# Recurrent attention and expert layers in one kernel: where the probabilities are loaded, and which engines do three small steps of the first unit

## The chip, the cores and the metric

The kernel runs on one core of one Trainium2 chip. The metric is the device time of one execution in microseconds (us), taken as the median of several runs. A core has five engines, each with its own in-order queue: PE (TensorE: matmuls; its weight loads are listed as PEld), DVE (VectorE), ACT (ScalarE), POOL (GpSimd) and SP (SyncE, which here only issues DMAs). DMAs from all queues run on the same 16 DMA engines.

## The reference

```python
# q, k, v, alpha: (4, 8, 768, 48) = batch, heads, time, head_dim
for t in range(S):
    state = alpha[:, :, t, :, None] * state + np.einsum('bhd,bhe->bhde', k[:, :, t], v[:, :, t])
    y[:, :, t] = np.einsum('bhd,bhde->bhe', q[:, :, t], state)
x = y.transpose(0, 2, 1, 3).reshape(3072, 384)
p = domain_probs / (domain_probs.sum(-1, keepdims=True) + 1e-09)      # (3072, 4)
for e in range(4):
    h = np.maximum(x @ w1[e], 0.0)                                    # w1[e]: 384 x 1024
    out += p[:, e:e + 1] * (h @ w2[e])                                # w2[e]: 1024 x 384
```

All is float32. A gated recurrence gives `x`; four expert layers are then applied to every row of it, and added with normalized probabilities as weights.

## The kernel before, in words

**Units.** The recurrence is cut into units of one batch and 128 time steps: 24 units, in the order of `units`. The generator `attention(u)` (L273) emits one unit in steps, one for each `yield`. Group 0 holds units 0 and 1; the later groups hold four each. When the units of a group are done, the expert layers run over their rows: `up` (L538 for group 0, L546 later) multiplies by `w1`, `down` (L637) by `w2`.

**One unit.** Alpha, k and q are loaded as rows (128 time steps on the partitions) and turned by PE transposes (L270, PSUM tile `tp`) into `AT` (copied by ACT, L281), `KT` (ACT, L286) and `QT`, which DVE multiplies by `AT` while reading PSUM (L293). The *own terms* are each step's product with itself: `t = q*k` (L289) and its sum over a head, `dot` (L290), which DVE writes onto the diagonal of `near` (L364). Then seven levels follow, for blocks of 1, 2, 4 ... 64 steps. In a level, `copy_q` copies the odd halves of `QT` into a block `qb` (two ACT copies, L312), `next_q` decays these halves in `QT` (DVE, L319) and forms the decays of the next level (DVE, L321), and `next_k` copies the odd halves of `KT` into the tile of the next level (L330, one copy of 128x256) while DVE writes the decayed even halves beside them (L331). The last level, 64, has no copy in `next_k`. PE forms the products of a level (`sc`, L338; `far`, L393, for level 64) and DVE takes them into `near` under a mask (`take`, L348). At the end `lat` is put together: two copies from `far` (ACT, L406), then two from `near` (ACT, L410), one for each half of the partitions. PE multiplies `lat` with the values (`yps`, L432), ACT copies the result into `xT` (L448), and PE forms the state for the next time steps from the turned keys (`turn_keys`, L456; `sps`, L467).

**Order at the start.** The order is written out by hand (`tc.manual_schedule()`, L721): every engine runs its instructions in the order in which they are emitted. ACT first issues three DMAs (L722 to L724): the identity, the masks, and the probabilities (`p_all`). SP issues the inputs of units 0 and 1 (`load(0, "akqv")`, `load(1, "akqv")`: a, k and q in one DMA each, L167, 192 KB; v in three, L172 to L174), then four pieces of the first expert's `w1` (`load_piece`, three DMAs each, L214 and L215). POOL clears tiles (L725 to L733). Then the steps of units 0 and 1 are emitted from a list of pairs (unit, n): one step of that unit, and `fill(n)` behind it, which puts n matmuls of zeros on PE (L747; each is two PE instructions). They need nothing that is still loading, and nothing reads what they give. `norm_probs` (L257 to L261) comes behind the list, and then the first `up`, for unit 0 alone. `load(after, ...)` inside a unit reloads its input tiles for a later unit; for unit 0 that is unit 2.

**Later.** A planner (`deal`, `cost`, `advance`) gives the steps of all later units due times among the matmuls of the expert layers; the change leaves it as it is.

Of the kernel before, what the change touches and what calls it, by code (L numbers as in the profile page):

```python
# [10 lines left out]
F32 = mybir.dt.float32  # L11
# [5 lines left out]
AX = mybir.AxisListType  # L17
# [3 lines left out]
def kernel(  # L21
# [37 lines left out]
    nc = tc.nc  # L59

    B, H, S, D = q.shape
    E, DM, F = moe_w1.shape
    P = 128
# [7 lines left out]
    NT = B * P  # L71
# [11 lines left out]
    n = np.arange(QUAD)[None, :]  # L83
# [7 lines left out]
    work = ctx.enter_context(tc.tile_pool(name="work", bufs=2))  # L91
# [7 lines left out]
    p_all = const.tile([P, NBLK, E], F32, name="p_all")  # L99
# [3 lines left out]
    near = const.tile([P, H, HALF], F32, name="near")  # L103
    lat = const.tile([P, H, P], F32, name="lat")
# [26 lines left out]
    def raw(u, nm):  # L131
        return values[u % 2] if nm == "v" else apart[nm] if u == 1 else early[nm]
# [27 lines left out]
    def load(u, names):  # L160
        if u >= len(units):
            return
        cb, b = units[u]
        for nm in names:
            src = srcs[nm][b, :, cb * P:(cb + 1) * P, :].rearrange("h s d -> s h d")
            if nm != "v":
                nc.sync.dma_start(out=raw(u, nm)[:, :, :D], in_=src)  # L167
                continue

            pairs = raw(u, nm).rearrange("p (a i) d -> p a i d", i=2)  # L170
            src = src.rearrange("p (a i) d -> p a i d", i=2)
            nc.sync.dma_start(out=pairs[:, :, 0, :D], in_=src[:, :, 0])  # L172
            nc.sync.dma_start(out=pairs[:, :, 1, :TAIL], in_=src[:, :, 1, QUAD:])
            nc.sync.dma_start(out=pairs[:, :, 1, TAIL:D], in_=src[:, :, 1, :QUAD])  # L174
# [13 lines left out]
    def load_piece(l, i, beside=False):  # L188
        if i >= E * NQ * LAST:
            return  # L190
        gi, k = divmod(i, E * NQ)
        e, c = divmod(k, NQ)
        if gi > l:
            w = wt[l][i] = wts.tile([P, 3, KC * QF], F32R, name=f"w{l + 1}",
                                    bufs=AHEAD if l == 0 else NQ)
            nc.sync.dma_start(out=w.bitcast(F32), in_=kept[l][k])
            return
        if l == 1 and not beside:
            return
        if l == 0:  # L200

            if gi > 0 or e == 0:
                shared[c] = wts.tile([P, 3, KC * QF], F32R, name="w2", bufs=NQ)
            w = shared[c][:, 2 - e % 2 if gi == 0 else 2].bitcast(F32)
        else:

            place = (hidden[c][:, 0] if not split2(gi, e, c) else hidden[c + NQ // 2][:, 1])
            w = place.rearrange("p f n -> p (f n)")[:, :KC * QF].bitcast(F32)
        wt[l][i] = w
        if l == 0:  # L210
            heads = moe_w1[e].rearrange("(h d) f -> h d f", d=D)[:, :, c * QF:(c + 1) * QF]
            w = w.rearrange("p (c f) -> p c f", f=QF)
            for part in range(2):
                nc.sync.dma_start(out=w[:, part], in_=heads[part * H // 2:(part + 1) * H // 2, :QUAD])  # L214
            nc.sync.dma_start(out=w[:, 2], in_=heads[:, QUAD:])  # L215
        else:
            nc.sync.dma_start(
                out=w.rearrange("p (c d) -> p c d", d=DM),
                in_=moe_w2[e].rearrange("(c p) d -> p c d", p=P)[:, c * FPQ:(c + 1) * FPQ])
# [44 lines left out]
    def halves(t, m):  # L264
        return t.rearrange("p a (b two r) -> p a b two r", two=2, r=m)

    def turned(src):
        tp = ps.tile([P, NP, P], F32, name="tp", tag="w")
        for p in range(NP):
            nc.tensor.transpose(tp[:, p, :], src(p), ident)  # L270
        return tp

    def attention(u):  # L273
        cb, b = units[u]
        ra, rk, rq, rv = (raw(u, nm) for nm in ("a", "k", "q", "v"))
# [6 lines left out]
        after = u + 2 if u == 0 else u + 1 if u > 1 else len(units)  # L282
# [1 line left out]
        yield  # L284
        KT = keys()
        nc.scalar.copy(out=KT, in_=turned(pair(rk)))  # L286
        own = work.tile([P, NT], F32, name="t")[:, :H * D].rearrange("p (h d) -> p h d", d=D)
        dot = work.tile([P, H], F32, name="dot")
        nc.vector.tensor_mul(own, rq[:, :, :D], rk[:, :, :D])  # L289
        nc.vector.reduce_sum(out=dot, in_=own, axis=AX.X)  # L290
        load(after, "k")
        yield
        nc.vector.tensor_mul(QT, turned(pair(rq)), AT)  # L293
        load(after, "q")
        yield

# [27 lines left out]
        def next_k(li):  # L324
            m = LEVELS[li]
            old = new = halves(KTs[li], m)
            if li + 1 < len(LEVELS):
                KTs.append(keys())
                new = halves(KTs[-1], m)
                nc.scalar.copy(out=new[:, :, :, 1, :], in_=old[:, :, :, 1, :])  # L330
            nc.vector.tensor_mul(new[:, :, :, 0, :], old[:, :, :, 0, :],  # L331
                                 spread(halved(decs[li])[:, :, :, 1], m))

# [70 lines left out]
        for s in range(2):  # L404
            rows = slice(HALF * s, HALF * (s + 1))
            nc.scalar.copy(out=parts[:HALF, :, s, :, HALF:], in_=far[rows])  # L406
        yield
        for s in range(2):
            rows = slice(HALF * s, HALF * (s + 1))
            nc.scalar.copy(out=lat[rows, :, rows], in_=near[rows])  # L410
        KT = KTs[-1]
        yield

# [49 lines left out]
        if cb < NCB - 1:  # L463
# [5 lines left out]
            for i in range(2):  # L469
                rows = slice(HD * i, HD * (i + 1))  # L470
                old, add = st[rows, :, i, :], sps[rows, :, i, :]
# [249 lines left out]
    with tc.manual_schedule():  # L721
        nc.scalar.dma_start(out=ident_all, in_=nc.inline_tensor(ident_np, name="ident_c").ap())  # L722
        nc.scalar.dma_start(out=masks, in_=nc.inline_tensor(mask_np, name="masks_c").ap())
        nc.scalar.dma_start(out=p_all, in_=moe_domain_probs.rearrange("(n p) e -> p n e", p=P))  # L724
        nc.gpsimd.memset(sts[B - 1], 0.0)  # L725
        for nm in "akq":
            for r in (early[nm], apart[nm]):
                nc.gpsimd.memset(r[:, :, D:], 0.0)
        nc.gpsimd.memset(lat[HALF:, :, :HALF], 0.0)
        for t in values + blocks:  # L730
            nc.gpsimd.memset(t, 0.0)
        for t in sts[:-1]:
            nc.gpsimd.memset(t, 0.0)  # L733

        load(0, "akqv")
        load(1, "akqv")
        for i in range(NQ):
            load_piece(0, i)

        idle = ps.tile([P, P], F32, name="idle", tag="g", bufs=4)
        zeros = sts[B - 1].rearrange("p a i d -> p (a i d)")[:, :P]

        def fill(n):
            for _ in range(n):
                nc.tensor.matmul(idle, lhsT=zeros, rhs=zeros, start=True, stop=True)  # L747

        runs = [attention(u) for u in range(len(groups[0]))]
        fill(8)  # L750
        for u, n in ((0, 3), (0, 6), (0, 4), (0, 5), (0, 5), (0, 4), (0, 3), (1, 0), (0, 0), (0, 2),
                     (0, 2), (1, 2), (0, 2), (1, 0), (0, 0), (0, 4), (0, 4), (0, 0)):
            next(runs[u])
            fill(n)
        norm_probs()

        span = cost(0, 0, 0) * FCH / 2 + cost(1, 0, 0)
        waiting.extend((span * (k + 1) / 15, u, runs[u])
                       for k, u in enumerate([1, 1, 1, 0, 1, 0, *[1] * 8]))
        for fc in range(FCH):  # L760
            up(0, 0, fc, slice(0, 1))
            advance(cost(0, 0, 0) / 2)
        down(0, 0, [0], deque())
        while waiting:
            next(waiting.popleft()[2], None)
        clock = 0.0
        waiting.extend((1.0 + k, 1, runs[1]) for k in range(2))
        waiting.extend(deal())

        for (gi, e), after in zip(tasks, [*tasks[1:], (None, None)]):  # L770
            rest = gi == e == 0
            for fc in range(FCH):
                up(gi, e, fc, slice(1, len(groups[0])) if rest else None)
                advance(cost(0, gi, e) / (2 if rest else 1))
            each = len(groups[gi]) if split2(gi, e) else 1
            turns = [range(k, k + each) for k in range(rest, len(groups[gi]), each)]
            for k, slots in enumerate(turns):

                between = deque()
                if after[1] == 0:  # L780
                    for step, at in enumerate((0.0, 0.6, 0.7, 0.78)):
                        at = at * len(turns) - k
                        if 0 <= at < 1:
                            between.append((at, lambda step=step: split_x(after[0], step)))
                down(gi, e, slots, between)
        while stores:
            stores.popleft()()
# [28 lines left out]
```

## Time and profile before

| what | value |
|---|---|
| median of 7 runs | 1068.43 us (1065.73 to 1070.2) |
| the profiled execution | 1068.02 us |
| its span, first to last instruction | 1066.3 us |
| mean granted TensorE clock | 0.998 |
| busy: PE, PEld, DVE, ACT, POOL | 98%, 85%, 73%, 53%, 3% |
| chain that ended last: PE, ACT, DVE, DMA | 85%, 5%, 4%, 3% |
| HBM read, written | 207.79 MB, 42.47 MB |

Busy shares are averages over the whole span. A row of the timeline gives the start from the span's beginning, the length, the engine, the line, and the tiles written and read; `[0.32 <-ACT lat L410]` behind it says that the engine stood idle for 0.32 us and what ended that. The chain of waits follows the work back from the last instruction, at each step to what released it. A queue is named q1 (DMAs issued by SP) or q10 (by ACT); its rows give packets, MB, and the time its packets took as a share of 16 DMA engines, which can exceed 100% since a DMA engine has more than one packet under way.

### The profile page before, as it was taken

What the parts mean: (1) busy time and instruction counts of PE and PEld (TensorE: products, weight loads), DVE (VectorE), ACT (ScalarE), POOL (GpSimd) and SP (SyncE); (2) the same over time, 40 slices, a digit from 0 to 9 for tenths busy, and PEclk for the clock granted to TensorE, in tenths of its full rate; (3) what the DMA queues carried; (4) which work ended last, traced back from release to release, by engine and by line L of the source; (5) the groups of instructions that cost most, each with busy time, mean ns of one, the idle gap of its engine ahead of it and who ended that gap; (6) DMA issues with size and microseconds to landing.
All of it is one profiled execution on the core that took longest, in us unless ns stands there. A gap on an engine that the chain in (4) does not pass through costs nothing.

```text
span 1066.3 us, 21598 instructions
## 1 busy us (share of the span) xinstructions
PE 1042.3 (98%) x8508; PEld 906.0 (85%) x8508; DVE 781.5 (73%) x1619; ACT 569.1 (53%) x1202; POOL 32.8 (3%) x71
## 2 busy tenths in 40 slices
PE   8899999999999999999999999999999999999998
PEld 7777776687877798898898998988989889898998
DVE  5488777667778777687876877976878776666565
ACT  5687875664756555536545535555564543423232
POOL 2010000000000000000000000000000000000000
PEclk9999999999999999999999999999999999999999
DMA  8596799797868958659569568495694554544531
GB/s 124 156 323 211 242 320 330 285 341 234 299 233 277 366 169 314 257 146 355 212 218 340 192 224 331 153 332 212 182 353 176 213 208 151 205 179 178 197 159 45
DMA packets 158837, 251.66 MB, mean 236 GB/s; under 512 B 120112, under 2 KB 135344, under 8 KB 136208
## 3 DMA queue, kind: packets, MB, share of 16 engines
q1 hardware_dynamic: 149600, 208.82, 57.6%
q0 software_dynamic: 5760, 41.29, 9.6%
q8 instruction: 67, 1.10, 0.4%
q10 hardware_dynamic: 3376, 0.17, 0.3%
q14 instruction: 34, 0.28, 0.1%
HBM read 207.79 MB, written 42.47 MB: 235 GB/s over the span
## 4 chain that ended last, share of the span: by engine, by line
PE 85%; ACT 5%; DVE 4%; DMA 3%; issue 2%; SPq 1%; ACTq 0%; DVEq 0%
PE ops L637 37%; PE one L546 22%; PE two L546 11%; PE sc L338 6%; PE yps L432 3%; PE tp L270 3%; ACT qb L312 2%; PE one L538 1%; PE far L393 1%; PE sps L467 1%; DMA hT<-in_moe_w_dram 1%; DVE w L230 1%; DMA rq<-in_q_dram 1%; ACT KT L330 1%; DVE near L348 1%
## 5 line engine op out<-in xcount | busy, mean ns | idle before, releaser
L637 PE MATMUL ops<-w,hT 128*128 128x384 f32 x1872 | 347.0, 340 | 0.4 <-DVE hT L564 0.4
L637 PEld LDWEIGHTS ops<-w,hT 128*128 128x128 f32 x1872 | 324.9, 188 | 4.9 <-DVE hT L564 0.7
L546 PE MATMUL one<-xT,w 128*128 128x512 f32 x960 | 253.7, 399 | 2.2 <-DVE xT L252 1.8
L546 PEld LDWEIGHTS one<-xT,w 128*128 128x128 f32 x960 | 176.2, 189 | 41.1 <-DVE xT L252 3.1
L557 ACT ACTIVATE t<-one 128x512 f32<-128x512 f32 (+1 forms) x192 | 107.1, 558 | 184.4 <-PE one L546 179.3
L312 ACT COPY qb<-QT 64x256 f32<-64x256 f32 x336 | 136.6, 407 | 73.4 <-DVE QT L293 44.7
L586 DVE SCALAR_TENSOR_TENSOR hT<-t,hT 128x512 fp32r<-128x512 f32 (+1 forms) x172 | 110.5, 643 | 68.7 <-ACT hT L584 66.5
L559 DVE TENSOR_TENSOR t<-t,two 128x512 f32<-128x512 f32 (+1 forms) x172 | 109.5, 636 | 58.5 <-ACT t L557 29.6
L584 ACT ACTIVATE hT<-t 128x512 fp32r<-128x512 f32 (+1 forms) x172 | 101.8, 592 | 86.1 <-DVE t L559 85.0
L546 PE MATMUL two<-xT,w 128*128 128x512 f32 x480 | 136.9, 394 | 0.0
L546 PEld LDWEIGHTS two<-xT,w 128*128 128x128 f32 x480 | 90.5, 189 | 20.2 <-DVE acc L666 0.3
L637 PE MATMUL ops<-hT 128*128 128x384 f32 x288 | 101.3, 492 | 3.7 <-DVE acc L666 3.2
L592 DVE SCALAR_TENSOR_TENSOR hT<-hT 128x512 fp32r<-128x512 f32 (+1 forms) x172 | 101.1, 636 | 0.0
L348 DVE COPY_PREDICATED near<-masks,sc 128x256 f32<-128x256 uint8 x144 | 77.0, 535 | 19.3 <-PE sc L338 16.5
L319 DVE TENSOR_TENSOR QT<-QT,dec 128x256 f32<-128x256 f32 x144 | 60.9, 423 | 36.0 <-ACT qb L312 35.3
L338 PEld LDWEIGHTS sc<-qb,KT 128*64 128x64 f32 x2304 | 72.7, 138 | 9.3 <-issue 4.7
L637 PEld LDWEIGHTS ops<-hT 128*128 128x128 f32 x288 | 51.8, 190 | 33.4 <-DVE acc L666 3.8
L338 PE MATMUL sc<-qb,KT 128*64 128x64 f32 x2304 | 77.2, 223 | 2.6 <-ACT qb L312 2.6
L666 DVE SCALAR_TENSOR_TENSOR acc<-ops,p_all,acc 128x384 f32<-128x384 f32 x82 | 50.1, 615 | 32.9 <-PE ops L637 31.8
L330 ACT COPY KT<-KT 128x256 f32<-128x256 f32 x144 | 60.0, 417 | 3.2
L331 DVE TENSOR_TENSOR KT<-KT,dec 128x256 f32<-128x256 f32 x144 | 60.2, 418 | 0.0
L538 PE MATMUL one<-xT,w 128*128 128x256 f32 (+1 forms) x240 | 46.2, 340 | 0.6 <-ACT xT L448 0.6
(88 smaller groups left out, 935.5 us busy)
## 6 DMA issues: line engine op xcount, KB each, us to landing
w<-kept SPq DMA_DIRECT2D x144, 1152.0 KB
kept<-w POOLq DMA_DIRECT2D x32, 1152.0 KB, 7.5
hT<-in_moe_w_dram SPq DMA_DIRECT2D x32, 384.0 KB
w<-in_moe_w_dram SPq DMA_DIRECT2D x48, 128.0 KB
ra<-in_alpha_dram SPq DMA_DIRECT2D x23, 192.0 KB
rk<-in_k_dram SPq DMA_DIRECT2D x23, 192.0 KB
rq<-in_q_dram SPq DMA_DIRECT2D x23, 192.0 KB
out_dram<-acc POOLq DMA_DIRECT2D x18, 192.0 KB, 7.6
```

Source lines behind the costliest of these rows:

```text
L312: nc.scalar.copy(out=qb[rows, :, i, :].rearrange("p a (b r) -> p a b r", r=m), in_=qv[rows])
L319: nc.vector.tensor_mul(qv, qv, spread(dv[:, :, :, 0], m))
L330: nc.scalar.copy(out=new[:, :, :, 1, :], in_=old[:, :, :, 1, :])
L338: nc.tensor.matmul(out[HALF * s:HALF * (s + 1), 2 * p:2 * p + 2, :], lhsT=KTs[li][:, p, HALF * s:HALF * (s + 1)], rhs=qbs[li][:, p, :, QUA ...
L348: nc.vector.copy_predicated(near.rearrange("p a (b two r) -> p a b two r", two=2, r=m)[:, :, :, 1, :], mk.unsqueeze(1).broadcast_to([P, H, ...
L546: nc.tensor.matmul(out, lhsT=w[:, part, kc], rhs=x_part(gi, part, kc), start=(part == terms[0] and kc == 0), stop=(part == terms[-1] and k ...
L557: nc.scalar.activation(out=t, in_=one, func=ACT.Copy, scale=FINE)
L559: nc.vector.tensor_add(t, t, two)
L584: nc.scalar.activation(out=top, in_=x, func=ACT.Relu, scale=TRIM)
L586: nc.vector.scalar_tensor_tensor(out=low, in0=x, scalar=0.0, in1=top.bitcast(F32), op0=ALU.max, op1=ALU.subtract)
L592: nc.vector.scalar_tensor_tensor(out=dif, in0=top.bitcast(F32), scalar=1 / 4096.0, in1=low.bitcast(F32), op0=ALU.mult, op1=ALU.subtract)
L637: nc.tensor.matmul(sums[at], lhsT=h, rhs=w, start=(n == begins[at]), stop=(n == ends[at]))
```

## The change

Four things differ, all at the start.

1. `p_all` is no longer loaded by ACT as its third DMA but by SP, behind the inputs of units 0 and 1 and ahead of the first weights.
2. For unit 0 alone (`alone`), the own terms are emitted behind the multiplication that gives `QT` instead of ahead of it, and with them the reload of k for unit 2.
3. For unit 0 alone, the copy in `next_k` runs on POOL instead of ACT (six copies), and the second of the two copies from `near` into `lat` on DVE instead of ACT.
4. Five fills fewer stand ahead of the queries' transposes: one ahead of the first step, one behind it and three behind the second.

```diff
-        own = work.tile([P, NT], F32, name="t")[:, :H * D].rearrange("p (h d) -> p h d", d=D)
         dot = work.tile([P, H], F32, name="dot")
-        nc.vector.tensor_mul(own, rq[:, :, :D], rk[:, :, :D])
-        nc.vector.reduce_sum(out=dot, in_=own, axis=AX.X)
-        load(after, "k")
+
+        def own_terms():
+            own = work.tile([P, NT], F32, name="t")[:, :H * D].rearrange("p (h d) -> p h d", d=D)
+            nc.vector.tensor_mul(own, rq[:, :, :D], rk[:, :, :D])
+            nc.vector.reduce_sum(out=dot, in_=own, axis=AX.X)
+            load(after, "k")
+
+
+        alone = u == 0
+        if not alone:
+            own_terms()
         yield
         nc.vector.tensor_mul(QT, turned(pair(rq)), AT)
+        if alone:
+            own_terms()
         load(after, "q")
...
-                nc.scalar.copy(out=new[:, :, :, 1, :], in_=old[:, :, :, 1, :])
+                copy = nc.gpsimd.tensor_copy if alone else nc.scalar.copy
+                copy(out=new[:, :, :, 1, :], in_=old[:, :, :, 1, :])
...
-            nc.scalar.copy(out=lat[rows, :, rows], in_=near[rows])
+            copy = nc.vector.tensor_copy if alone and s else nc.scalar.copy
+            copy(out=lat[rows, :, rows], in_=near[rows])
...
-        nc.scalar.dma_start(out=p_all, in_=moe_domain_probs.rearrange("(n p) e -> p n e", p=P))
...
         load(1, "akqv")
+        nc.sync.dma_start(out=p_all, in_=moe_domain_probs.rearrange("(n p) e -> p n e", p=P))
         for i in range(NQ):
             load_piece(0, i)
...
-        fill(8)
-        for u, n in ((0, 3), (0, 6), (0, 4), (0, 5), (0, 5), (0, 4), (0, 3), (1, 0), (0, 0), (0, 2),
+        fill(7)
+        for u, n in ((0, 2), (0, 3), (0, 4), (0, 5), (0, 5), (0, 4), (0, 3), (1, 0), (0, 0), (0, 2),
                      (0, 2), (1, 2), (0, 2), (1, 0), (0, 0), (0, 4), (0, 4), (0, 0)):
```

## The prediction

> **What bounds the kernel now.** I read the page's busy shares first, then busy times by stage, then the chain of work from 0 to 80 us, then the DMA queues and the instructions in order of time for the first 30 us. The stages (columns: length; busy us of PE, PEld, DVE, ACT, POOL; granted clock; DMA share; GB/s):
>
> ```profile
> 0.00:26.54 26.54, 22.24 (x269) 20.92 (x269) 13.95 (x39) 14.03 (x30) 5.92 (x21) 1.00 0.86 124
> 26.54:66.00 39.46, 34.38 (x368) 27.86 (x369) 24.18 (x57) 27.76 (x67) 1.74 (x3) 1.00 0.71 212
> ...
> 180.00:1066.30 886.30, 878.15 (x6866) 774.64 (x6861) 654.82 (x1330) 443.64 (x922) 17.11 (x32) 1.00 0.65 235
> ```
>
> From 180 us on PE is busy for 878.15 of 886.30 us: nothing in this change touches that work. Before 26.54 us most of PE's busy time is the idle matmuls of L747, which no result needs. The first real product (L538) starts at 26.54, when unit 0's attention is done. So the change is worth what it takes off these 26.54 us, if the rest only moves. The chain there (start, length, what):
>
> ```profile
> 1.86 6.97 DMA rq<-in_q_dram
> ...
> 9.52 0.13 DVE dot L290
> 9.65 0.34 issue
> 9.99 0.69 DVE QT L293
> ...
> 23.56 0.62 ACT lat L410
> 24.18 0.01 issue
> 24.19 0.62 ACT lat L410
> 24.81 0.04 issue
> 24.86 1.12 PE yps L432 x32
> ```
>
> See three things: until 8.83 all waits for unit 0's queries; QT then waits until 9.99 behind unit 0's own terms (L289, L290), though its transposes (8.96, 0.63 long) end at 9.59; and at the end two `lat` copies run one after the other on ACT.
>
> **The loads.** The probabilities are 3072 rows of 16 bytes. In 4 to 7 us the queues carried (packets, MB, share of 16 engines):
>
> ```profile
> q1 hardware_dynamic: 1295, 0.25, 77.3%
> q10 hardware_dynamic: 2751, 0.04, 75.3%
> ```
>
> q10 is ACT's queue, and these 2751 packets are the probabilities; q1 is SP's, with rk and rq. In 9 to 12 us q1 is alone:
>
> ```profile
> q1 hardware_dynamic: 2416, 0.46, 145.4%
> ```
>
> That is 0.25 MB in 3 us against 0.46. The trace's semaphore increments give landings: ra 4.45, rk 6.23, rq 8.83, the probabilities 9.17, then unit 1's a, k, q at 10.35, 11.54 and 12.74, that is one 192 KB load per 1.2 us when q1 is alone. ra does not move (the probabilities' first packets come at 3.9 us, when its data is through). So rk moves to 4.45 + 1.2 = 5.65 and rq to 6.85. Bounds for rq: 6.85 and, if the probabilities did not hold it up, 8.83. I take 6.85, from the same transfer on the same queue.
>
> **PE up to QT.** One fill is two instructions. One fill less ahead of ra gives nothing, since tp ra starts (PEld 4.57) just after ra's landing. Behind it 4 idle instructions instead of 6 (0.83 us, 0.14 each) bring rk's transposes from 6.36 to about 5.9; these take 0.47 to the next; then 6 instead of 12 (1.50 us) take 0.75, so rq's transposes start at about 7.07, not 8.96, behind rq's 6.85. They end at 7.70. With own terms behind it QT starts there: 9.99 - 7.70 = 2.29 us.
>
> **Own terms.** 0.56 (L289) + 0.55 (L290) now stand between QT (0.68) and L319 of level 0 on DVE: free at 7.70 + 0.68 + 1.02 (they overlap by some 0.05 each) = 9.40. L319 waits for two qb copies anyway (10.77 to 11.63 before, so 8.48 to 9.34): its start moves from 11.67 to 9.40, **-2.27**. The cover is those copies; without it the 1.1 us would be on the path. `dot` is read only by `near` (15.27 before). The load of unit 2's k now waits for an L289 that runs 8.4 to 9.0, about when it ran before (8.93); SP comes to that load only after twelve weight issues, at 23.82, so nothing stands behind this wait.
>
> **K copies to GpSimd.** Level 0 now, in order of time (start, length, engine, line, what):
>
> ```profile
> 11.66 0.45 ACT L330 COPY KT<-KT 128x256 f32<-128x256 f32 x1
> 11.67 0.43 DVE L319 TENSOR_TENSOR QT<-QT,AT 128x256 f32<-128x256 f32 x1 [0.99 <-ACT qb L312]
> ...
> 12.18 0.87 ACT L312 COPY qb<-QT 64x256 f32<-64x256 f32 x2
> ```
>
> The ACT copy lies beside L319, and the next qb waits for L319: taking it off ACT shortens nothing in levels 0 to 2. From 14.45 to 19.94 DVE is packed end to end (near, takes, L319), so ACT is not what ends last either. Only ahead of `far`: qb of level 6 starts at 20.11 behind L330 (19.32) and unit 1's KT copy (19.63); without L330 it starts at 19.98, when L319 (19.52, 0.42) is done: **-0.13**.
>
> The price: six GpSimd copies of 128x256. No copy on GpSimd is in this trace; its rows are memsets:
>
> ```profile
> 3.56 1.93 POOL L731 MEMSET qb<- 128x512 f32 x4
> ```
>
> 128x512 takes 0.54, 128x128 0.20, so 128x256 lies at 0.31; reading as well as writing bounds it at twice that, 0.62. The first can run at 7.2, when KT is copied and GpSimd is done with memsets (6.58). Each of the others has until the L331 after next, 2.4 us later, so its length alone is hidden. No row shows GpSimd and VectorE at work together, so I bound the interference: nothing, or GpSimd's time taken whole from VectorE in all five, 5 x 0.62 less the gaps VectorE has behind L331 of levels 0 and 1 (12.77 to 13.08, 14.05 to 14.45, 0.71 together) = 2.4 us. I take 0.31: two copies fall into those gaps, the third meets `near` (15.27) right behind L331, the last two meet takes, which read PSUM. Value **+0.31**.
>
> [...]
>
> **The last copy on VectorE.** It stands behind L331 (23.42 to 23.84). It takes 0.36 (64x192 of L473) to 0.69 (128x512 of L364), so it ends at 24.2 to 24.5, not 24.81. But PE comes free late as well:
>
> ```profile
> 24.86 1.08 PE L432 MATMUL yps<-lat,rv 128*32 128x128 f32 x32 [0.32 <-ACT lat L410]
> ```
>
> PE waited only 0.32 us, behind idle matmuls that stay. So **-0.32** at most, and I take it; with 0.69 it is -0.28.
>
> **The moved issue.** ACT's queue loses an issue of 0.59 us. SP gets it ahead of twelve weight loads (first issue 12.27). SP runs ahead of the data: the first weight packets end at 13.75, when unit 1's inputs are through. The same packets lie ahead of the weights as before, so the fourth piece (landed 29.6) stays there to within 0.6. Its reader, the seventh fc of L538, started at 31.18 and would start at 28.8; but the sps matmuls behind it waited 1.28 us for ACT at 33.21, so a stall until 29.6 fits in. The probabilities are read at 23.76 (L257), now 21.4, and land at about 15.
>
> **Sum.** -2.27 - 0.13 - 0.32 + 0.31 = -2.41. After 26.54 loads are issued when PE or ACT frees their tiles, and move with them. The profiled execution took 1068.02 (span 1066.3 and 1.7 around it), 0.41 under the median 1068.43; 1065.6 there, **1066.0** as a median.
>
> **Rivals.**
> - *The weights come late.* If the probabilities push the weights by the 2.0 us by which they held up rq (8.83 - 6.85), the seventh fc waits until 31.6, and after its 0.75 us PE reaches sps at 32.4 instead of 30.8: 1.6 lost, 1067.6. For it: DMA runs at 0.2 to 0.4 of its share from 13.5 to 25 and never catches up. Against: the inputs ahead are through earlier by as much.
> - *rq lands no earlier*, because SP's own issue of it (1.86, 1.18 long) sets it. Then only 0.40 (dot), 0.13 and 0.32 are left, less 0.31: 1067.9. Against: q1's halved packets.
> - *GpSimd stalls VectorE* in the levels (L319, L331, near), the case on the slower side. With a hold of h the cost is 5h - 0.71 against a gain of 2.72: even at h = 0.69, over 0.2% slower from h = 1.11; at 1.3 us it is 5.8 - 2.7 = +3.1, 1071.5. Against: memsets of twice the size take 0.54.
> - *The clock.* From 168.9 to 172.3 it was 0.5, after PE had waited 0.83 us twice on DVE's splits (L252). Moved work may escape this, 3.4 x 0.5 = 1.7 us more: 1064.3.
>
> **Numbers.** Forecast 0.60 (1065.0 to 1067.2; 0.45 of it beyond 0.2%, 0.15 within), weights late 0.12, rq no earlier 0.10, clock 0.10, GpSimd 0.08. Over 0.2% (2.1 us, about what a measurement of this kernel can tell from no change) faster: 0.45 + 0.10 = 0.55; within: 0.15 + 0.12 + 0.10 = 0.37; slower: 0.08. The range reaches from the clock case to the late rivals with the median's spread, 1064.2 to 1068.3, and leaves out the GpSimd case and part of the tails.
>
> **What would show it.** rq's transposes near 7.1 and QT near 7.7; L319 of level 0 near 9.4; POOL copies under 0.62 us and L319, L331, near at 0.42 and 0.68 as before; yps with no wait; the first L538 near 24.1. Wrong if rq still lands after 8 us, if near or L319 grow beside POOL, or if L538 waits for a DMA.

## The result and the profile after

| | before | after |
|---|---|---|
| median of the runs made side by side, us | 1068.02 (29 runs, 1065.47 to 1070.2) | 1064.1 (11 runs, 1063.27 to 1066.03) |
| ratio | | 0.9968 [0.9959, 0.9976] |
| profiled execution, us (its span) | 1068.02 (1066.3) | 1065.58 (1063.8) |

The change makes the kernel faster, by 0.32%. The ratio is estimated over all runs and is not the quotient of the two medians, which is 0.9963. Two sizes stand for the one change: the profiled executions differ by 2.44 us (2.5 in the span; the forecast's sum was 2.41), the medians by 3.9. The forecast median of 1066.0 is 1.9 above the measured one, and 1064.1 lies 0.1 below the low end of the range; the ratio times 1068.43, from which the forecast started, is 1065.0. What the 1.5 us between the two sizes has to do with the clock near 167 us stands with e7 and e8 below.

Where the profiled 2.5 us arise, read from the starts (us) of the same work in the two timelines:

| work | before | after | gained so far |
|---|---|---|---|
| rq lands (semaphore record) | 8.83 | 6.65 | 2.18 |
| rq's transposes | 8.96 | 7.46 | 1.50 |
| `QT` of the first step | 9.99 | 8.17 | 1.82 |
| `QT` of level 0 (L319, now L328) | 11.67 | 9.86 | 1.81 |
| `far` (L403 after) | 20.97 | 19.37 | 1.60 |
| `yps` (L432, now L443) | 24.86 | 22.94 | 1.92 |
| first L538, now L549 | 26.54 | 24.61 | 1.93 |
| first sps (L467, now L478) | 33.21 | 31.14 | 2.07 |
| second `up` product of unit 0's blocks | 65.18 | 62.78 | 2.40 |
| end of the span | 1066.3 | 1063.8 | 2.5 |

So 1.8 us are gained by `QT`, 0.2 lost again in the levels, 0.3 gained at `yps`, and 0.47 gained behind the first L549, where the forecast had nothing. The stages, with the cut moved by what the start gained (length; busy us of PE, PEld, DVE, ACT, POOL; granted clock; DMA share; GB/s):

```profile
0.00:24.61 24.61, 21.49 (x259) 20.55 (x259) 14.68 (x40) 11.20 (x23) 8.69 (x27) 1.00 0.80 115
24.61:64.00 39.39, 35.36 (x370) 28.35 (x371) 24.58 (x57) 27.54 (x67) 1.74 (x3) 1.00 0.73 223
177.30:1063.80 886.50, 878.45 (x6894) 775.42 (x6890) 655.48 (x1331) 443.69 (x923) 17.12 (x32) 1.00 0.65 235
```

In the first row ACT is busy for 11.20 us instead of 14.03, POOL for 8.69 instead of 5.92: the K copies and, on ACT, the second `lat` copy too. The last row, from where 886.50 us remain, has PE busy for 878.45; the last 886.50 us of before have 878.35. Next to nothing there moved but its start.

The loads first. In 4 to 7 us only SP's queue carries anything (packets, MB, share of 16 engines):

```profile
q1 hardware_dynamic: 3064, 0.48, 150.7%
```

It now moves 0.48 MB where it moved 0.25 beside the probabilities. Then the timeline, from the transposes of rk on:

```profile
6.07 0.88 PE L270 MATMUL tp<-ident,rk 128*128 128x128 f32 x4
...
7.46 0.60 PE L270 MATMUL tp<-ident,rq 128*128 128x128 f32 x4
...
8.17 0.69 DVE L300 TENSOR_TENSOR QT<-tp,AT 128x512 f32<-128x512 f32 x1 [8.17 <-PE tp L270]
8.78 0.55 DVE L291 TENSOR_TENSOR t<-rq,rk 128x384 f32<-128x384 f32 x1
```

`QT` waits for PE's transposes alone now, and the own terms (L291) follow it. But rk's transposes take 0.88 us where the same four took 0.63 before: the granted clock rose to full at 6.64 us in this execution, and at 5.08 in that of before. These moments are the trace's first clock records; the column of the stages counts the time ahead of them as 1.00, so the rise does not show there. It shows in the idle matmuls: one of their instructions takes 0.24 us at the start (3.35 us for 14) and 0.14 once the clock is up (0.83 for 6). That is the first step that came out otherwise than worked out.

### The profile page after: what moved, and what is told of

Read it like the earlier page. It is cut to its first block, busy times and chain, and to the rows that moved or that the text cites. A ratio compares the mean times of both kernels' runs of the same rounds, so it can differ in the third digit from the quotient of the medians.

```text
span 1063.8 us, 21578 instructions
## 1 busy us (share of the span) xinstructions
PE 1041.7 (98%) x8498; PEld 905.6 (85%) x8498; DVE 782.2 (74%) x1620; ACT 565.5 (53%) x1195; POOL 35.5 (3%) x77
## 4 chain that ended last, share of the span: by engine, by line
PE 85%; ACT 5%; DVE 4%; DMA 2%; issue 2%; SPq 1%; POOL 0%; ACTq 0%; DVEq 0%; POOLq 0%
PE ops L648 36%; PE one L557 22%; PE two L557 11%; PE sc L348 6%; PE yps L443 3%; PE tp L270 3%; DMA hT<-in_moe_w_dram 2%; ACT qb L321 2%; PE one L549 1%; PE far L403 1%; PE sps L478 1%; SPq L214 1%; DMA w<-in_moe_w_dram 1%; DVE w L230 1%; DVE near L358 1%
## 5 line engine op out<-in xcount | busy, mean ns | idle before, releaser
L328 DVE TENSOR_TENSOR QT<-QT,dec 128x256 f32<-128x256 f32 x144 | 61.2, 425 | 36.1 <-ACT qb L321 35.4
L340 ACT COPY KT<-KT 128x256 f32<-128x256 f32 x138 | 57.5, 416 | 3.0
L549 PE MATMUL one<-xT,w 128*128 128x256 f32 (+1 forms) x240 | 46.7, 341 | 1.2 <-ACT xT L459 0.6
```

What stands on the lines that cost most here:

```text
L328: nc.vector.tensor_mul(qv, qv, spread(dv[:, :, :, 0], m))
```

## The experiments

The times of the work named (us from the span's start), from one profile each; "clock up" is when the granted clock rose to 1.0:

| kernel | clock up | rq's transposes | `QT` | `QT` level 0 | `far` | `yps` | first L538/L549 | sps | second `up` |
|---|---|---|---|---|---|---|---|---|---|
| before | 5.08 | 8.96 | 9.99 | 11.67 | 20.97 | 24.86 | 26.54 | 33.21 | 65.18 |
| after | 6.64 | 7.46 | 8.17 | 9.86 | 19.37 | 22.94 | 24.61 | 31.14 | 62.78 |
| e1 | 4.20 | 7.73 | 8.44 | 10.11 | 19.41 | 23.29 | 24.97 | 31.64 | 63.61 |
| e2 | 5.75 | 9.07 | 9.81 | 11.51 | 21.04 | 24.61 | 26.27 | 32.81 | 64.44 |
| e3 | 6.91 | 7.59 | 8.30 | 9.99 | 19.29 | 22.87 | 24.53 | 31.05 | 63.01 |
| e4 | 7.39 | 7.82 | 8.53 | 10.20 | 19.71 | 23.27 | 24.94 | 31.47 | 63.11 |
| e5 | 6.97 | 7.62 | 8.33 | 10.01 | 19.52 | 23.40 | 25.08 | 31.76 | 63.42 |
| e6 | 6.64 | 7.67 | 8.39 | 10.09 | 19.61 | 23.18 | 24.85 | 31.40 | 63.06 |
| e7 | 6.23 | 7.37 | 8.08 | 9.76 | 19.28 | 22.85 | 24.52 | 31.08 | 62.72 |
| e8 | 7.20 | 8.84 | 9.86 | 11.52 | 20.82 | 24.71 | 26.39 | 33.05 | 65.03 |
| e9 | 4.57 | 6.68 | 7.42 | 9.11 | 18.33 | 21.90 | 23.57 | 30.55 | 62.08 |
| e10 | 6.47 | 7.50 | 8.21 | 9.91 | 19.21 | 22.80 | 24.46 | 30.99 | 62.63 |
| e11 | 6.13 | 8.52 | 9.54 | 11.22 | 20.53 | 24.41 | 26.09 | 32.76 | 64.39 |
| e12 | 6.72 | 7.50 | 8.21 | 9.90 | 19.13 | 22.85 | 24.52 | 31.06 | 62.71 |

The single runs of one kernel spread by 1.4 to 4.7 us, so parts of some tenths are read from differences inside one profile (from one piece of work to a later one), which come out alike to some 0.04 us from kernel to kernel wherever the change under test isn't between them. e1 to e4 ran together on one chip (before there: 1066.8 us, 33 runs), e5 to e8 on a second (1066.79, 31 runs), e9 to e12 on a third (1067.36, 27 runs).

### e1: the probabilities alone

Before, with nothing but the load moved:

```diff
-        nc.scalar.dma_start(out=p_all, in_=moe_domain_probs.rearrange("(n p) e -> p n e", p=P))
...
         load(1, "akqv")
+        nc.sync.dma_start(out=p_all, in_=moe_domain_probs.rearrange("(n p) e -> p n e", p=P))
```

> The kernel before with one edit: the probabilities' load moved from ACT's queue to SP's, behind the inputs of units 0 and 1. Theory (the probabilities' packets held up the queries): rq lands at 6.7 us instead of 8.8; its transposes then stand behind twelve idle instructions and start at 7.9 to 8.3, QT at about 8.6, the first L538 at 25.1 instead of 26.5, so 1.4 us less than before (ratio 0.9987). Rival (SP's own issue sets rq's landing): rq lands after 8 us and L538 stays within 0.3 us of 26.5.

Measured: 1066.08 us, ratio 0.9991 [0.9982, 1.0]; in the profile rq lands at 6.97 instead of 8.83, and the first L538 stands at 24.97 instead of 26.54, 1.57 earlier. rq's transposes start at 7.73 behind the old number of idle matmuls, and `QT` follows 0.71 later, as in the changed kernel, although the own terms still stand ahead of it.

### e2: everything but the probabilities

The changed kernel, with the load of the probabilities back on ACT's queue (the reverse of e1's edit).

> The kernel after with the probabilities' load put back on ACT. Theory: rq lands at 8.8 again, its transposes start at 8.9, QT at 9.6 (the own terms no longer stand ahead of it), L319 of level 0 at 11.3, the first L538 at 26.1 against 24.6 after: 1.5 us slower than after. Rival (the fewer fills and the other edits make the gain): L538 stays under 25.

Measured: 1066.05 us, 0.999 [0.9981, 0.9999]; first L549 at 26.27, 0.27 earlier than before. rq's transposes are at 9.07 again. By the profiles 1.57 of the 1.93 us at the first L549 are the load's (1.66 from e2 to after), and the two parts add up (1.57 + 0.27 = 1.84) but for what the clock's rise shifts. That the medians of e1 and e2 are equal says little: their intervals are 1.9 us wide.

No run takes the fewer fills alone, and the clock hides their share here. e1 and e9, whose clocks rose early and at nearly the same moment (4.20 and 4.57), start rq's transposes at 7.73 and 6.68: 1.05 us lie between the old and the new number of idle matmuls, with the load moved in both. After, with its clock up at 6.64, is ahead of e1 by only 0.27 there. So the shares hold for these profiles and not for every execution.

### e3 and e5: the copies back on ACT, one kind at a time

e3:

```diff
-                copy = nc.gpsimd.tensor_copy if alone else nc.scalar.copy
+                copy = nc.scalar.copy
                 copy(out=new[:, :, :, 1, :], in_=old[:, :, :, 1, :])
```

> The kernel after with the six K copies of unit 0 back on ACT. Theory (GpSimd and VectorE hold each other up): L319 of levels 1 and 3 go back from 0.52 and 0.62 to 0.43 us, the far products start 0.3 earlier for that and 0.13 later for ACT's copy, so L538 starts at 24.4 instead of 24.6: 0.2 us faster than after. Rival (the copies on GpSimd shorten the chain): L538 at 24.8 or later. Too little for the times; the profile decides.

e5:

```diff
-            copy = nc.vector.tensor_copy if alone and s else nc.scalar.copy
+            copy = nc.scalar.copy
             copy(out=lat[rows, :, rows], in_=near[rows])
```

> The kernel after with both copies from near into lat on ACT again. Theory: yps starts 0.3 us later against the chain ahead of it (22.94 becomes 23.25) and L538 at 24.9. Rival (the idle matmuls ahead of yps set it): L538 stays at 24.6.

Measured: e3 1065.45 us, 0.9982 [0.9973, 0.9991]; e5 1065.66, 0.9976 [0.9965, 0.9987]. From `QT` of level 0 to `far` e3 takes 9.30 us, as before and e1 do; after, e2, e4 and e5 take 9.51 to 9.53. So the GpSimd copies cost 0.21 there. The timelines show where. After, on VectorE at levels 1 and 3, and GpSimd's copies below it:

```profile
11.27 0.52 DVE L328 TENSOR_TENSOR QT<-QT,dec 128x256 f32<-128x256 f32 x1 [0.31 <-ACT qb L321]
...
13.54 0.69 DVE L374 TENSOR_TENSOR near<-ident,dot 128x512 f32<-128x512 f32 x1
14.14 0.62 DVE L328 TENSOR_TENSOR QT<-QT,dec 128x256 f32<-128x256 f32 x1
```

```profile
11.09 0.41 POOL L340 COPY KT<-KT 128x256 f32<-128x256 f32 x1 [3.04 <-DVE KT L341]
12.45 0.40 POOL L340 COPY KT<-KT 128x256 f32<-128x256 f32 x1 [0.95 <-DVE KT L341]
13.75 0.73 POOL L340 COPY KT<-KT 128x256 f32<-128x256 f32 x1 [0.90 <-DVE KT L341]
15.35 0.40 POOL L340 COPY KT<-KT 128x256 f32<-128x256 f32 x1 [0.87 <-PE sc L348]
17.43 0.40 POOL L340 COPY KT<-KT 128x256 f32<-128x256 f32 x1 [1.68 <-DVE KT L341]
```

The same two of VectorE's instructions at level 3 in e3:

```profile
13.58 0.69 DVE L374 TENSOR_TENSOR near<-ident,dot 128x512 f32<-128x512 f32 x1
14.18 0.42 DVE L328 TENSOR_TENSOR QT<-QT,dec 128x256 f32<-128x256 f32 x1
```

The copy issued at 13.75 meets `near`, takes 0.73 instead of 0.40, and the product behind `near` takes 0.62 instead of 0.42. At level 1 a copy at 11.09 meets L328, which takes 0.52 instead of the 0.43 of e3. The copies at 15.35 and 17.43 lie beside the takes and cost nobody anything: they take 0.40, and the two pairs of takes 1.49 and 0.89, where e3 has 1.49 and 0.90. `near` and L328 have two SBUF inputs; the takes read one of theirs from PSUM. When L328 started, 0.23 us of the copy were left at level 1 (11.09 + 0.41 - 11.27), 0.12 at level 2 and 0.34 at level 3; L328 grew by 0.09, nothing and 0.20, that is by what was left less some 0.14.

From `far` to `yps`: 3.89 before, 3.88 in e1 and e5, 3.56 to 3.58 in after, e2, e3 and e4. So the `lat` copy on VectorE gains 0.31 (a copy of 0.42 us), and it does so with or without the K copies. In after the idle matmuls ahead of `yps` end at 22.94, the moment it starts, so that they set this gain.

### e4: the own terms ahead of `QT`

```diff
-        alone = u == 0
-        if not alone:
-            own_terms()
+        alone = u == 0
+        own_terms()
         yield
         nc.vector.tensor_mul(QT, turned(pair(rq)), AT)
-        if alone:
-            own_terms()
```

> The kernel after with unit 0's own terms ahead of QT again. Theory: with rq landed at 6.65 the own terms (1.1 us) end by 7.9, before rq's transposes do (8.1), so QT stays at 8.2 and L538 at 24.6: nothing lost, the edit is worth nothing by itself once the probabilities are out of the way. Rival (what the prediction counted): QT 0.4 us later, L538 at 25.0.

Measured: 1064.49 us, 0.9981 [0.9972, 0.999]. From rq's transposes to `QT` it takes 0.71 us, exactly as after. VectorE's own rows in e4:

```profile
6.67 0.56 DVE L291 TENSOR_TENSOR t<-rq,rk 128x384 f32<-128x384 f32 x1 [6.67 <-DMA rq<-in_q_dram]
...
8.53 0.69 DVE L299 TENSOR_TENSOR QT<-tp,AT 128x512 f32<-128x512 f32 x1 [0.71 <-PE tp L270]
```

By their starts alone `QT` (8.53) and the first product (24.94) look like the rival. But the lateness is there before the own terms can matter: the clock rose at 7.39 in this execution, and rq's transposes start 0.36 us later than in after. The own terms start at rq's landing and are over by 7.8, while PE comes to rq's transposes only at 7.82: VectorE idles 0.71 us ahead of `QT` even so. With the load moved and PE this late, the edit gains nothing. It gains where VectorE comes last: before had 1.03 from the transposes to `QT`, e2 has 0.74. Where PE is early (transposes at 6.68 and `QT` at 7.42 in e9) terms that end at 7.8 would be in the way again by some 0.3 (an estimate from these starts); that was not tried.

### e6: eight idle matmul pairs at the start

The forecast had `QT` at 7.70 and it came at 8.17. Either the fill that was taken away lets the clock rise later, or the moment of the rise is chance. e6 is the changed kernel with `fill(7)` back at `fill(8)`.

> The kernel after with eight fills at the start instead of seven. In the profile after, the granted clock reached 1.0 at 6.6 us instead of 5.1. Theory (the one fill less, with PE waiting for ra, delayed the clock): full clock at 5.1 again, rk's transposes take 0.63 instead of 0.88, QT starts at 7.8 instead of 8.2 and L538 at 24.2. Rival (when the clock rises is chance): full clock anywhere from 5 to 7 us, whatever the fills.

Measured: 1065.36 us, 0.9985 [0.9976, 0.9993]; the clock rose at 6.64 us, to the hundredth where it did with seven. The theory of the missing fill falls. Over the 14 profiles of this case the rise lies anywhere from 4.20 to 7.39 us (4.20 to 7.20 in the five with eight fills, 4.57 to 7.39 in the nine with seven), and from there on whole multiples of 3.413 us lie between one change of the clock and the next (47, 48, 261, 262, 309 and 310 of them were met, and one in each fall; 48 in before, from 5.08 to 168.92, and 47 in after, from 6.64 to 167.06). What sets the moment of the rise no run shows.

### e7 and e8: idle matmuls where the clock falls

In both profiles PE waits 0.82 or 0.83 us twice (ahead of 168.41 us in before, of 166.66 in after), and the clock is down just behind. In after (columns as for the stages):

```profile
165.00:166.00 1.00, 0.51 (x1) 0.19 (x1) 0.96 (x3) 0.00 (x0) 0.00 (x0) 1.00 1.02 433
166.00:167.00 1.00, 0.34 (x2) 0.30 (x3) 0.96 (x3) 0.00 (x0) 0.54 (x1) 1.00 1.04 442
167.00:168.00 1.00, 1.00 (x4) 0.81 (x3) 1.00 (x5) 0.00 (x0) 0.00 (x0) 0.53 1.01 424
168.00:169.00 1.00, 1.00 (x3) 0.78 (x3) 0.61 (x2) 0.55 (x1) 0.10 (x1) 0.50 1.00 424
```

PE is busy for 0.85 of the 2 us from 165 on; then the clock is at 0.5 for 3.41 us, worth 3.41 x 0.5 = 1.7. e7 (of after) and e8 (of before) put idle matmuls into these waits, ahead of the matmul in the split branch of `up`:

```diff
+                        if gi == 1 and e == 0 and fc == 0 and part == 1 and kc > 0:
+                            for _ in range(3):
+                                nc.tensor.matmul(two[:, :P], lhsT=ident, rhs=ident, start=True, stop=True)
```

> The kernel after with three idle matmuls ahead of each of the two first products of group 1 that wait for VectorE's splits (twice 0.8 us, near 165 us). Theory (the waits let the granted clock fall to 0.5 for 3.4 us in some runs and not in others): mean clock 1.00 in every run, spans near 1062, 1.0 us less than after as a median. Rival (the clock falls for another reason, or it costs nothing): clock 0.998 in half the runs, median unchanged.

> The kernel before with the same idle matmuls. Theory: mean clock 1.00 in every run; its spans then are 1.9 us (the later start of L538) to 2.5 us (the difference of the two profiles) over those of the kernel after with the same matmuls, so near 1064.2, and the rest of the difference of the medians was the clock. Rival (the change gains more than its start): 3 us or more over the kernel after with them.

Measured: e7 1064.36 us, 0.9975 [0.9966, 0.9985]; e8 1066.72, 0.9998 [0.9989, 1.0007]. e7's same stretch:

```profile
165.00:166.00 1.00, 0.99 (x7) 0.93 (x7) 1.00 (x2) 0.00 (x0) 0.00 (x0) 1.00 1.02 433
166.00:167.00 1.00, 0.84 (x5) 0.57 (x4) 0.97 (x3) 0.00 (x0) 0.55 (x1) 1.00 1.00 424
167.00:168.00 1.00, 1.00 (x6) 0.81 (x5) 1.00 (x5) 0.42 (x1) 0.00 (x0) 1.00 1.02 433
168.00:169.00 1.00, 1.00 (x9) 0.84 (x7) 0.96 (x3) 0.18 (x1) 0.41 (x1) 1.00 1.05 442
```

The clock stays up there, and e7's runs lie within 1.44 us (1063.6 to 1065.04) where after's spread over 2.76. Not every run has a mean clock of 1.000, as the theory had it: 4 of e7's 9 stand at 0.999, and of e8's 11 four at 0.999 and two at 0.998. A 0.999 need not be the fall near 166 us, which alone makes 0.998 of the mean (1.7 of 1064 us): in e7's profiled run, one of the four, the clock is up from 6.23 to 1060.95 us and falls behind the last matmul, which ends at 1058.69. The two at 0.998 have no trace and stay unexplained.

Every run has a mean granted clock, and the runs of before on these three chips fall into groups by it: at 1.000, medians of 1066.26, 1066.26 and 1066.78 us (38 runs); at 0.998, 1068.06, 1068.23 and 1069.08 (46 runs); 7 lie at 0.999. So the groups lie 1.8 to 2.3 us apart, near the 1.7 of one fall, and about half of the runs of before stand at 0.998. After has both groups too (1063.69 at 1.000 in 5 runs, 1065.57 at 0.998 in 5). Taken by groups, and across sessions, the change gains 2.6 to 3.1 us with the clock at 1.000 and 2.5 to 3.5 at 0.998; between e8 and e7, of which only two runs stand at 0.998, the medians differ by 1066.72 - 1064.36 = 2.36. That brings the profiled 2.4 and the medians' 3.9 together in part: the medians of the first comparison may mix these groups in different shares (its runs of before have no clock on record). e7's median is not below after's 1064.1, which was taken in another session; that the fall is worth removing was therefore not shown in a median, only the narrower spread.

In which executions it falls can be set against a grid of 3.413 us laid from each trace's first clock record on (e6 has the multiples that were met; that it also goes on where no change near 166 us marks it, in e1, e2, e9 and e11, is the author's assumption). In the seven profiles that have the fall (before, after, e3 to e6, e10) it comes at the end of a stretch of the grid in which both waits lie whole, and PE was busy for 0.46 to 0.54 of it (1.57 of 3.41 us in before, 1.58 in after). In e2, e9 and e11, which have the waits and no fall, an edge of the grid lies between the two or in the start of the second (166.18 in e2, between them), and PE is busy for at least 0.65 of either stretch; in e1 the waits lie in one stretch but for 0.05 us, the first is 0.67 us long (in e3, where the clock fell, 0.48), PE is busy for 1.97 of 3.41, and the clock stays up. How little work is too little these runs do not settle: PE was busy for 1.66 of the 3.41 us from 336.18 in before, and nothing fell.

### e9: GpSimd copies only beside the takes

```diff
-                copy = nc.gpsimd.tensor_copy if alone else nc.scalar.copy
+                copy = nc.gpsimd.tensor_copy if alone and li >= 4 else nc.scalar.copy
```

> The kernel after with GpSimd's K copies in levels 4 and 5 only; levels 0 to 3 are copied by ACT. Theory (only the copies that meet L319 and near hold VectorE up, those beside the takes are free and relieve ACT ahead of the far products): L319 of levels 1 and 3 at 0.43, far 9.17 us behind L319 of level 0 (9.51 after, 9.30 with all copies on ACT), L538 0.3 us earlier than after; the state copy still follows sps by 1.17 us, since VectorE has waited for GpSimd before. Rival: far stays at 9.5 behind L319.

Measured: 1064.37 us, 0.9972 [0.9962, 0.9981]. From `QT` of level 0 to `far` 9.22 us instead of 9.51: 0.29 gained (and 0.08 less than with all copies on ACT), with VectorE's L328 back at 0.43 in level 1 and 0.42 in level 3, and both GpSimd copies at 0.40. This execution also had an early clock (4.57), so its rq transposes started at 6.68, just behind rq's landing, and its first L549 at 23.57. That shows what is late next. PE's rows in e9:

```profile
29.51 0.49 PE L549 MATMUL one<-xT,w 128*128 128x128 f32 x2 [1.00 <-DMA w<-in_moe_w_dram]
30.23 0.49 PE L549 MATMUL one<-xT,w 128*128 128x128 f32 x2 [0.23 <-DMA w<-in_moe_w_dram]
30.55 1.03 PE L478 MATMUL sps<-rv,AT 128*128 128x96 f32 x8
```

The weights hold PE for 1.23 us, and sps comes 6.98 us after the first L549 instead of 6.53: of an earlier start of 1.04 us, 0.59 arrive at sps.

### e10 and e11: the gain behind the first L549

Between sps and the second `up`, 31.97 us of before had become 31.64, with nothing edited in between. The table parts the kernels in two: 31.96 to 31.98 in before, e1, e3 and e8, 31.53 to 31.66 in after, e2, e4 to e7, e9 and e12, which are those with K copies on GpSimd. The state's copy behind sps, before:

```profile
33.21 1.13 PE L467 MATMUL sps<-rv,AT 128*128 128x96 f32 x8 [1.28 <-ACT AT L456]
```

```profile
34.86 0.72 DVE L473 COPY st<-sps 64x192 f32<-64x192 f32 x2 [1.25 <-PE sps L467]
```

and after:

```profile
31.14 1.13 PE L478 MATMUL sps<-rv,AT 128*128 128x96 f32 x8
```

```profile
32.31 0.72 DVE L484 COPY st<-sps 64x192 f32<-64x192 f32 x2 [0.77 <-PE sps L478]
```

The copy starts 1.65 us after sps's start before, and 1.17 after. The instructions of that line in before hold one that is no copy:

```profile
L473 DVEq EVENT_SEMAPHORE  x3: 21/21/21, 34.4 to 88.9; - x3
```

The state tile was cleared by POOL in the preamble (the loop at L743 after), so VectorE's first write to it has two waits, for PE and for POOL, and the second stands in an instruction of its own: at 34.4, when sps has ended (33.21 + 1.13), with the copy 0.48 behind it. In the changed kernel VectorE has waited for later work of POOL long before (its K copies), and the extra instruction is gone. The rival was the `lat` copy or the lighter ACT. Both e10 (after, with the K copies on ACT as in e3) and e11 (before) clear these tiles on VectorE:

```diff
         for t in sts[:-1]:
-            nc.gpsimd.memset(t, 0.0)
+            nc.vector.memset(t, 0.0)
```

> The kernel after with all K copies on ACT and the three state tiles cleared by VectorE instead of GpSimd. Theory (with the copies on ACT the first state copy needs two waits, for PE and for GpSimd's clearing, and starts 1.65 us behind sps instead of 1.17; the copies on GpSimd had taken the second wait away): 1.17 us here, though no copy is on GpSimd, and the second stage of up (128x256) 0.5 us earlier than with the copies on ACT alone, measured from the first L538 (38.0 instead of 38.5). Rival (GpSimd's copies shift something else): 1.65 stays.

> The kernel before with the three state tiles cleared by VectorE instead of GpSimd, nothing else. Theory (two waits on one instruction cost 0.5 us): the state copy 1.17 us behind sps instead of 1.65, second stage of up 38.2 us behind the first L538 instead of 38.6, 0.5 us off the time (ratio 0.9995, too little to be told from no change by the times). Rival: 1.65 and 38.6 stay.

Measured: e10 1064.64 us, 0.9972 [0.9964, 0.9981]; e11 1066.71, 0.9994 [0.9985, 1.0002]. e11, with no other edit of the change:

```profile
33.93 0.72 DVE L473 COPY st<-sps 64x192 f32<-64x192 f32 x2 [0.77 <-PE sps L467]
```

sps stands at 32.76 there, so the copy is 1.17 behind it, and 31.63 us lie from sps to the second `up`; e10 has 31.64. With no K copy on GpSimd the 0.33 are had all the same: the second wait is their cause, and the copies only took it away by the way. (The forecast had all of the copy's 0.48 arrive at the second `up`; 0.33 do.) So the K copies on GpSimd cost 0.21 us ahead of `far` and give 0.33 behind sps, which clearing the tiles on VectorE gives without them.

The other 0.14 us lie between the first L549 and sps: 6.66 to 6.68 in before, e1, e5, e8 and e11, 6.52 to 6.56 in after, e2, e3, e4, e6, e7, e10 and e12. They go with the `lat` copy on VectorE. They arise at ACT's first `qb` copy of unit 1, which starts 1.94 us behind the first L538 or L549 in the first five kernels and 1.81 or 1.82 in all others; why it starts earlier there was not tried.

### e12: the pieces together

e9 and e7 together, with one fill less ahead of `yps`:

```diff
-                     (0, 2), (1, 2), (0, 2), (1, 0), (0, 0), (0, 4), (0, 4), (0, 0)):
+                     (0, 2), (1, 2), (0, 2), (1, 0), (0, 0), (0, 4), (0, 3), (0, 0)):
```

> The kernel after with what the runs point to: GpSimd's K copies in levels 4 and 5 only (0.34), one fill less ahead of yps (up to 0.2), and three idle matmuls ahead of each of the two products of group 1 that wait for VectorE (no fall of the clock near 165 us in any run). Theory: L538 at 24.2, spans near 1061.5, 1 us under after where its clock falls and 0.5 where it does not; ratio to before near 0.9965. Rival: within 0.3 us of after.

Measured: 1063.81 us (1062.85 to 1064.24, 5 runs), 0.9965 [0.9952, 0.9978]. The lowest median of all kernels and the narrowest spread, but against the kernel before it can't be told from after (0.9968 [0.9959, 0.9976]). The first L549 is at 24.52, not 24.2. The fill less brought nothing: from `far` to `yps` it takes 3.72 instead of 3.57. PE was through with its idle matmuls at 22.48 and VectorE's `lat` copy at 22.44, but `yps` starts only at 22.85. With the copies on two engines an event-semaphore instruction more stands ahead of `yps` on PE: one in before (at 22.5), two in after (22.7 and 22.8) and in e12 (22.48 and 22.74); in the whole trace that line has five in after and e12, four in e5 with both copies on ACT. That this second wait costs the 0.37, as one did on VectorE, is likely and was not tested.

## Why the prediction was right, step by step

- **The loads**: right. rq lands at 6.65 for a forecast 6.85, and e1 shows that this one edit brings 1.57 of the 1.93 us. The rival "rq lands no earlier" falls with it.
- **PE up to `QT`**: the term "-2.27" is mis-sized; it measured -1.81 at level 0 (11.67 to 9.86). The step that failed is "these take 0.47 to the next": the walk took durations from a profile whose clock was up at 5.08 us. With the rise at 6.64 rk's transposes take 0.88 (0.72 to the next) and the four idle instructions ahead of them 1.06 instead of 0.56, so rq's start at 7.46, not 7.07. The rest of the 0.47 by which `QT` is late (8.17, not 7.70) is the step from the transposes' end to `QT` (8.06 to 8.17), which the sum put at nothing. This 0.47 is nearly the whole miss at the first L549 (24.61 for 24.1). e6 shows that the edit did not set that rise; with the rise at 4.57 (e9) rq's transposes came at 6.68 and `QT` at 7.42, earlier than forecast.
- **Own terms**: right that the `qb` copies hide them (1.68 us from `QT` to level 0 before, 1.69 after); but e4 shows that the edit has no share in the gain with rq early and PE late as here, since the terms end before PE comes to the transposes. The forecast had not priced it apart from the load.
- **K copies**: "-0.13" and "+0.31" came as +0.21 net, for +0.18. e9 parts them: without the copies that meet VectorE it is -0.08 (9.22 for 9.30), so the meetings cost 0.29, the 0.09 and 0.20 of the two rows. The place was right (the copy beside `near`), and the takes were free as forecast (1.49 and 0.89 us for two pairs, 1.49 and 0.90 without the copies), though no row had shown that then. Left out was level 1, where a copy was to fall into a gap and met L328 by 0.09; the one meeting that was counted came at 0.20, on the product behind `near`, not on `near` itself (0.69 for 0.68). That 0.31 and 0.29 lie so close is in part luck. And "no row shows GpSimd and VectorE at work together" is true of copies only: GpSimd's DMA issues stand beside VectorE's work from 53.56 us on.
- **`lat` on VectorE**: "-0.32" measured -0.31.
- **The weights**: right that a stall there would be covered. PE waits for `w` in after:

```profile
30.09 1.06 PE L549 MATMUL one<-xT,w 128*128 128x128 f32 x4 [0.54 <-DMA w<-in_moe_w_dram]
```

  and sps at 31.14 still gained 2.07. e9 shows where the cover ends.
- **"After 26.54 ... move with them"**: missed a gain of 0.47: 0.33 from the state's copy (e10, e11), 0.14 not settled. By luck it makes up for the 0.46 lost at `QT`, so that the sum came out right, -2.5 for -2.41, with two of its terms wrong.
- **The clock**: the rival "moved work may escape this" gets no clear verdict: the fall shifts from 168.9 to 167.1 in the profiles and stays as long. What was missed is that before itself seems to have it in about half of its runs, so a median carries a share of 1.7 us by chance; most of the 1.9 us between the forecast median and the measured one may be that.

## What to carry to other kernels

A load of 3072 rows of 16 bytes on one queue held up the loads that the first work needs, though those were on another queue (rq landed 1.86 us earlier in e1 and 2.18 in after): issue such a load behind those. When costs of tenths at a kernel's start are worked out from one trace, look first when its clock rose, and give the sum the spread of that moment (4.20 to 7.39 us here). And where an engine's first touch of a tile carries a second wait, let the engine that uses the tile also clear it (0.33 us in e11).

## What the runs showed of the hardware

- The second wait of a VectorE copy cost 0.48 us at its place: an event-semaphore instruction at 34.4, the copy at 34.86 (before); with one wait (e11) the copy starts 1.17 us after sps's start instead of 1.65.
- GpSimd copied 128x256 of fp32 in 0.40 to 0.42 us, and in 0.73 when it met VectorE's `near`, with two SBUF inputs, already at work (0.69, as in e3 without the copies). L328, also with two, took 0.09 us, nothing and 0.20 more when it started with 0.23, 0.12 and 0.34 us of a copy left. Beside the takes, with one input in PSUM, two copies took 0.40 each.
- Behind two waits of PE close together (0.48 to 0.83 us, then 0.82 or 0.83) the granted clock fell to 0.5 for 3.41 us in seven of the eleven profiles that have no idle matmuls there, and not in the other four; with three idle matmuls in each wait it stayed up at that place in three profiles of three.
